# Sixty-eight columns transposed instead of 128, sixteen low halves made by DMA, and a re-costed planner in a fused attention + two-MLP kernel

## The chip, the cores and the metric

The kernel runs on one core of a Trainium2 chip. The metric is the device time of one execution in microseconds (us). Three runs of the kernel before gave 583.89, 578.93 and 583.06 us, median 583.06. A profile is one more execution, recorded instruction by instruction; its own time was 584.52 us, of which 582.6 us is the span from its first to its last instruction.

## The reference

Inputs are q, k, v of shape (2, 8, 768, 64) and four weight matrices. In short:

```
scores = q @ k^T / 8            # 2 batches, 8 heads, 768 x 768
keep   = (key < 4) | (0 <= query - key < 128)        # 4 sinks, a window of 128
x = softmax(where(keep, scores, -1e9)) @ v           # -> 1536 tokens x 512
h = x @ w_in1 ; x = (h * clip(h + 3, 0, 6) / 6) @ w_out1     # 512 -> 2048 -> 512
h = x @ w_in2 ; y = (h * sigmoid(1.702 h)) @ w_out2          # 512 -> 2048 -> 512
```

All inputs and outputs are float32. The weights are converted on the chip and every product of the MLPs is made of three products of rounded parts (high x high, high x low, low x high).

## The kernel before, in words

**Attention.** 1536 tokens are 12 tiles of 128 queries. A tile has two "duos" of four heads each (`duo`). Of one head a tile looks at 196 keys: 128 in the middle and a second part of 68 (64 of the window's ends plus 4 sinks). For a duo PE makes the scores (L1152), DVE adds the mask and takes the row's minimum of the negated scores (L1167, with a short read of the accumulator), ACT takes the exponential in place in a tile `pexp` (L1175, likewise two records), DVE makes the inverse sums (L1183, L1184), and DVE or ACT scales `pexp` (L1194, L1192). Then PE transposes: one "turn" (`turn`, L1203) turns two heads with four 128x128 transposes into one PSUM bank, and one copy of 128x512 (L442 on ACT, L444 on DVE) brings it to `pts` in SBUF. There are 48 turns. The tile `pexp` has 256 columns before; its last 60 are zeroed once at the start (L1100). `tile_values` multiplies by v (L1226 the 128 keys, L1234 the 68) and writes the result as a high part (ACT) and a low part (DVE, L1253) into `xy`.

**MLPs.** The work is a list of items; an item is one block of 512 tokens and one slice f of 128 hidden columns. Item i has an "up" (12 matmuls of 512 columns, L932) and a "down" (12 more, L980). The first layer's items come in the order of `BLOCKS`: tokens 0 to 511 with f 0 to 7 (items 0 to 7), tokens 512 to 1023 with f 0 to 7 (items 8 to 15), then f 8 to 15 of the same two blocks (items 16 to 31), then the last block. The second layer follows (items as before, then a part in a form with fewer products, L616 and L732). An item's activation is L944 on ACT and L949 on DVE, its split into high and low L442 or L444 and L565.

**Weights.** A slice f of both matrices arrives by a 1 MB DMA into one of two `stage` buffers and is converted by ACT (L472) and four DVE steps (L477, L485, L493, L500). The load of slice f+2 can start only when L500 of slice f has released the buffer. For each item W_in and W_out are then split: the high part is a cast (L442 on ACT or L444 on DVE), the low part is weight minus high part, a subtraction on DVE (L550): tile `w0l` for W_in, tile `wg` for W_out. The rings of W_out's high and low parts (`w1h`, `w1l`) have two buffers each, so the parts for item i can be made only when the down of item i-2 has finished.

**What sets the order.** A planner (`Plan.issue`) goes through all operations with an assumed cost for each on each engine that may do it, and writes every engine's instructions out in the order that it finds. On the chip an engine works strictly in that order. DMAs with accumulation are issued by POOL; before the change they are used only in the last part (L680, L824), with an assumed latency ADD_DMA of 4500 ns.

Of the kernel before, what the change touches and what calls it, by code (L numbers as in the profile page):

```python
# [9 lines left out]
F32 = mybir.dt.float32  # L10
# [4 lines left out]
ALU = mybir.AluOpType  # L15
PSUM = bass.MemoryType.PSUM

P = 128
SINKS = 4
HALF = 64  # L20
# [15 lines left out]
SLACK = 50  # L36
ISSUE = 1300
ADD_DMA = 4500
PACT = 0.15
PDVE = 0.5  # L40
STRETCH = 1.0
# [12 lines left out]
PX = 8  # L54
# [13 lines left out]
def tile_sink_window_attention_moe_moe2(  # L68
# [10 lines left out]
    nc = tc.nc  # L79
    B, S, H, D = 2, 768, 8, 64  # L80
    NTOK, DM = out.shape
    NF = w1.shape[0]
# [7 lines left out]
    TAIL = HALF + SINKS  # L90

    W = P + TAIL
# [81 lines left out]
    ident = const.tile([P, P], F32, name="ident")  # L174
# [58 lines left out]
    with tc.tile_pool(name="msk", bufs=1) as mp:  # L233
# [18 lines left out]
            out=out, in0=grid, scalar1=x, scalar2=LOW, op0=op, op1=ALU.mult  # L252
# [187 lines left out]
    def copy(eng, out, in_):  # L440
        if eng is nc.scalar:
            eng.copy(out, in_)  # L442
        else:
            eng.tensor_copy(out, in_)  # L444
# [20 lines left out]
    def plan_convert(plan, f, due):  # L465

        st, w = plan.stage[f % len(stage)], plan.wf[f]
        wd = st.tile.rearrange("p (n t) -> p n t", t=2)
        low, top = wd[:, :, 0], wd[:, :, 1]
        plan.op(  # L470
            [("ACT", 1036)],
            lambda e: e.activation(w.tile.bitcast(F32), top.bitcast(F32), AF.Abs),  # L472
            due, reads=[st], writes=[w], chain="abs",
        )
        plan.op(
            [("DVE", 602)],
            lambda e: e.tensor_scalar(  # L477
                out=w.tile.bitcast(F32), in0=w.tile.bitcast(F32), scalar1=TOP_LO, scalar2=TOP_HI,
                op0=ALU.max, op1=ALU.min,
            ),  # L480
            due, writes=[w],
        )
        plan.op(
            [("DVE", 602)],
            lambda e: e.tensor_scalar(  # L485
                out=w.tile, in0=w.tile, scalar1=3, scalar2=0x3FFFFFF8,
                op0=ALU.logical_shift_left, op1=ALU.bitwise_and,
            ),
            due, writes=[w],
        )  # L490
        plan.op(
            [("DVE", 1135)],
            lambda e: e.scalar_tensor_tensor(  # L493
                out=w.tile, in0=top, scalar=-0x40000000, in1=w.tile, op0=ALU.bitwise_and, op1=ALU.bitwise_or
            ),
            due, reads=[st], writes=[w],
        )
        plan.op(
            [("DVE", 1135)],
            lambda e: e.scalar_tensor_tensor(  # L500
                out=w.tile, in0=low, scalar=29, in1=w.tile, op0=ALU.logical_shift_right, op1=ALU.bitwise_or
            ),
            due, reads=[st], writes=[w],
        )


    def plan_mlps(plan, blocks, item_due, late=None):
# [13 lines left out]
        second = len(items) - NF  # L521
# [7 lines left out]

        def split(i, part):  # L530
            f = items[i][3]
            return split_of(plan.wf[f], slice(512 * part, 512 * (part + 1)), f"w{part}", part, i >= second - NF + 4)

        def split_of(src, cols, cls, part=0, act=True):
            hi, lo = Buf(cls=cls + "h"), Buf(cls=cls + "l")
            n = cols.stop - cols.start
            at = (slice(None), slice(None)) if part else (slice(None), slice(0, n))

            def of():
                x = src.tile if src.tile.dtype == F32 else src.tile.bitcast(F32)  # L540
                return parted(x[:, cols]) if part else x[:, cols]

            full = n == 512
            opts = [("ACT", 520 if full else 300)] + ([] if act else [("DVE", 335)])
            plan.op(
                opts, lambda e: copy(e, hi.tile[at], of()), None, reads=[src], writes=[hi], chain=f"split{part}",
            )
            plan.op(
                [("DVE", 602 if full else 335)],
                lambda e: e.tensor_tensor(  # L550
                    out=lo.tile[at], in0=of(), in1=hi.tile[at].bitcast(F32), op=ALU.subtract
                ),
                None, reads=[src, hi], writes=[lo],
            )
            return hi, lo
# [485 lines left out]
        for i in range(len(items)):  # L1041
            f = items[i][3]
# [9 lines left out]
            if second <= i < second + NF:  # L1052
                f = i - second
# [36 lines left out]
    def plan_attention(plan, pool, due):  # L1090
# [4 lines left out]
        kept = [pool.tile([P, KQ], F32, name="kept", tag=f"kept{j}") for j in range(KEPT)]  # L1095
        for T in range(EARLY, NTILE):
            kqt[T] = kept[T % KEPT]
        pexps = [pool.tile([P, 2 * P], F32, name="pexp", tag=f"pexp{k}") for k in range(PX)]
        for t in pexps:
            nc.scalar.mul(t[:, W:], ident[:, W - P :], 0.0)  # L1100
        plan.ring("pexp", PX, lambda k: pexps[k])
        top, low = slice(0, HALF), slice(HALF, P)
        both = slice(0, P)
# [1 line left out]
        kq_b = [Buf(kqt[T], at=landed.get(("kq", T))) for T in range(EARLY + KEPT)]  # L1105
# [16 lines left out]
        def duo(d, pts):  # L1122

            T, half = divmod(d, 2)
            i = tok[T][1]
            kind = min(i, 2)
            front = T - 1 if i else T
            when = None
            sc = [Buf(cls="bank", kind="s") for j in range(2)]
            nbs, z = [Buf(cls="nb") for _ in range(4)], Buf(cls="z")  # L1130
            pes = [Buf(cls="pexp") for _ in range(4)]

            def scores(e):
# [22 lines left out]
                                )  # L1156

            plan.op(
                [("PE", 1050)], scores, when, reads=[kq_b[t] for t in sorted({front, T})], writes=sc, chain="scores",
            )  # L1160
            heads = [(a, j) for a in range(2) for j in range(2)]
            for a, j in heads:
                n = 2 * a + j
                cols = slice(a * W, (a + 1) * W)
                plan.op(
                    [("DVE", 283)],
                    lambda e, j=j, n=n, cols=cols: e.tensor_tensor_reduce(  # L1167
                        out=pes[n].tile[:, :W], in0=sc[j].tile[:, cols], in1=masks[kind],
                        scale=-SCALE, scalar=LOWEST, op0=ALU.add, op1=ALU.min, accum_out=nbs[n].tile,
                    ),  # L1170
                    when, reads=[sc[j], mask_b[kind]], writes=[pes[n], nbs[n]],
                )
                plan.op(
                    [("ACT", 410)],
                    lambda e, n=n: e.activation(  # L1175
                        pes[n].tile[:, :W], pes[n].tile[:, :W], AF.Exp,
                        bias=nbs[n].tile, scale=-1.0, accum_out=z.tile[:, n : n + 1],
                    ),
                    when, reads=[nbs[n]], writes=[pes[n]], adds=[z], chain="exp",
                )  # L1180
# [16 lines left out]
            for a in range(2):  # L1197
                pt, pb = Buf(cls="bank", kind="t"), Buf(cls="pts")

                def turn(e, a=a, pt=pt):  # L1200
                    for n in range(4):
                        j, x = divmod(n, 2)
                        e.transpose(  # L1203
                            pt.tile[:, n * P : (n + 1) * P], pes[2 * a + j].tile[:, x * P : (x + 1) * P], ident
                        )

                plan.op([("PE", 440)], turn, when, reads=pes[2 * a : 2 * a + 2], writes=[pt], chain="turn")
                plan.op(
                    [("ACT", 478), ("DVE", 602)],
                    lambda e, pt=pt, pb=pb: copy(e, pb.tile, pt.tile.rearrange("p (n t) -> p n t", t=P)),  # L1210
                    when, reads=[pt], writes=[pb],
                )
                pts.append(pb)

        def tile_values(T, pts):
# [6 lines left out]
            def values(e):  # L1222
                for hp in range(NPAIR):
                    p = pts[hp].tile
                    for j in range(2):
                        e.matmul(  # L1226
                            av.tile[j * D : (j + 1) * D, hp * P : (hp + 1) * P],
                            rows.tile[:, 2 * hp + j, :], p[:, 2 * j, :],
                            start=(hp == 0), stop=False, skip_group_check=True,
                        )  # L1230
                    for c in range(2):
                        for j in range(2):
                            o = hp * P + c * HALF
                            e.matmul(  # L1234
                                av.tile[j * D : (j + 1) * D, o : o + HALF],
                                halves_of[c].tile[:TAIL, c, 2 * hp + j, :],
                                p[:TAIL, 2 * j + 1, c * HALF : (c + 1) * HALF],
                                start=False, stop=True, skip_group_check=True,
                            )

            plan.op(
                [("PE", 2000)], values, when, reads=list(dict.fromkeys([rows] + halves_of)) + pts, writes=[av],
            )
            blk, off = divmod(T, 4)
            dst = (slice(None), off // 2, slice(None), slice(off % 2 * P, (off % 2 + 1) * P))
# [15 lines left out]
        for T in range(NTILE):  # L1261
            pts = []
# [7 lines left out]
    def fast_path():  # L1270
        with tc.manual_schedule(), tc.tile_pool(name="mlp", bufs=1) as pool, tc.tile_pool(
# [23 lines left out]
            def limit(b, slots, o):  # L1295
# [15 lines left out]
                    return free > (1 - mine if v or t else 2 - mine)  # L1311
                if b.kind == "v":
                    return v == 0 or free > 2
                if b.kind == "t":

                    return t + sum(1 for x in plan.slots["pts"] if x is not None and x.left) < NPT
# [186 lines left out]
```

## Time and profile before

| | before |
|---|---|
| runs | 583.89, 578.93, 583.06 us; median 583.06 |
| profiled execution | 584.52 us; span 582.6 us |
| PE busy | 563.2 us (97%) |
| DVE busy | 456.8 us (78%) |
| ACT busy | 389.4 us (67%) |
| POOL busy | 54.2 us (9%) |
| first matmul of an up | 42.6 us |
| up of item 8 begins | 114.9 us |
| up of item 16 begins | 165.2 us |
| last turn and values of the attention end | about 213 us |

PE is a pipeline: the busy time of one matmul contains its passage through the array, so neighbours overlap, and a busy share of 97% does not say that nothing waits. The share is an average over a span in which the work changes: attention alone at first, then attention together with the first MLP's items, then MLP alone. What a saving on another engine is worth depends on the stage in which it falls.

### The profile page before, as it was taken

The numbers are of one execution on the slowest core, as the hardware profiler recorded it, in microseconds if no ns is written. First come the engines' busy times: TensorE is split into PE (matmuls) and PEld (weight loads), VectorE is DVE, ScalarE is ACT, GpSimd is POOL, SyncE is SP. The second block draws the span as 40 slices with busy tenths as digits, with TensorE's granted clock in tenths as the row PEclk, the third lists the DMA queues.
The fourth block names the chain that finished last, engine by engine and source line by source line (L and its number), as shares of the span: only waits on it lengthen the run. The fifth ranks groups of instructions, "written<-read, shape, count | busy, mean of one in ns | idle before, by whom it ended". The sixth has DMA issues, their size and how long they took to land.

```text
span 582.6 us, 11436 instructions
## 1 busy us (share of the span) xinstructions
PE 563.2 (97%) x4482; PEld 496.6 (85%) x4482; DVE 456.8 (78%) x951; ACT 389.4 (67%) x803; POOL 54.2 (9%) x62
## 2 busy tenths in 40 slices
PE   6989989999999999999999999999999999999996
PEld 6868867788788888888888888888888888999995
DVE  6799979998996556559999999993456665667784
ACT  5898756984746665457655678454478788768762
POOL 0000000000000000000000000000002344765000
PEclk9799999999999999999999999999999999999998
DMA  8984464145342000000445440420024567999512
GB/s 256 364 249 161 124 201 164 44 145 186 111 168 74 1 2 1 1 0 1 151 168 186 147 145 1 144 74 1 0 78 77 82 95 145 168 184 198 99 38 77
DMA packets 23468, 65.65 MB, mean 113 GB/s; under 512 B 2480, under 2 KB 10672, under 8 KB 19312
## 3 DMA queue, kind: packets, MB, share of 16 engines
q1 hardware_dynamic: 13360, 51.22, 26.7%
q0 software_dynamic: 10048, 13.63, 14.8%
q8 instruction: 37, 0.61, 0.4%
q14 instruction: 23, 0.19, 0.1%
HBM read 47.02 MB, written 3.15 MB: 86 GB/s over the span
## 4 chain that ended last, share of the span: by engine, by line
PE 80%; DVE 9%; ACT 4%; DMA 3%; issue 1%; DVEq 0%; SPq 0%
PE bank L980 24%; PE bank L932 24%; PE bank L732 13%; PE bank L616 13%; DMA stage<-in_w_dram 3%; PE bank L1203 2%; ACT pexp L1175 2%; PE bank L1152 2%; PE bank L1226 2%; DVE wf L500 1%; DVE wf L493 1%; PE bank L1234 1%; DVE pexp L1167 1%; DVE wg L550 1%; DVE wf L485 1%
## 5 line engine op out<-in xcount | busy, mean ns | idle before, releaser
L980 PE MATMUL bank<-wg 128*128 128x512 f32 x768 | 190.0, 382 | 2.7 <-ACT wg L442 2.5
L980 PEld LDWEIGHTS bank<-wg 128*128 128x128 f32 x768 | 143.3, 189 | 24.7 <-ACT wg L442 3.2
L932 PE MATMUL bank<-xy,w0h 128*128 128x512 f32 x512 | 154.1, 382 | 1.5 <-DVE xy L1253 1.0
L932 PEld LDWEIGHTS bank<-xy,w0h 128*128 128x128 f32 x512 | 95.5, 189 | 15.3 <-DVE xy L1253 1.3
L932 PE MATMUL bank<-xy,w0l 128*128 128x512 f32 x256 | 97.0, 379 | 0.0
L680 POOL DMA_DIRECT2D wf<-wf x24 | 29.0, 1287 | 469.2 <-ACT wf L661 433.9
L442 ACT CAST wg<-wf 128x512 fp32r<-128x512 f32 x78 | 48.2, 618 | 31.9 <-PE bank L980 24.4
L944 ACT ACTIVATE u<-bank,three 128x512 f32<-128x512 f32 x48 | 32.8, 684 | 39.4 <-PE bank L932 39.3
L550 DVE TENSOR_TENSOR w0l<-wf,w0h 128x512 fp32r<-128x512 f32 x72 | 49.2, 684 | 11.6 <-ACT w0h L442 11.4
L550 DVE TENSOR_TENSOR wg<-wf,wg 128x512 fp32r<-128x512 f32 x64 | 43.9, 685 | 15.3 <-ACT wg L442 15.3
L932 PEld LDWEIGHTS bank<-xy,w0l 128*128 128x128 f32 x256 | 48.4, 189 | 6.8
L949 DVE SCALAR_TENSOR_TENSOR u<-u,bank 128x512 f32<-128x512 f32 x48 | 32.7, 681 | 24.3 <-ACT u L944 24.1
L1175 ACT ACTIVATE pexp<-pexp,nb 128x196 f32<-128x196 f32 x96 | 42.9, 450 | 9.2 <-DVE nb L1167 8.9
L472 ACT ACTIVATE wf<-stage 128x1024 f32<-128x1024 f32 x32 | 37.8, 1182 | 16.2 <-DMA stage<-in_w_dram 12.9
L442 ACT CAST wg<-u 128x512 fp32r<-128x512 f32 x59 | 36.6, 620 | 14.3 <-DVE u L949 14.3
L565 DVE TENSOR_TENSOR wg<-u,wg 128x512 fp32r<-128x512 f32 x64 | 43.9, 685 | 0.9
L493 DVE SCALAR_TENSOR_TENSOR wf<-stage,wf 128x1024 int32<-128x1024 int32 x32 | 39.1, 1221 | 0.4
L500 DVE SCALAR_TENSOR_TENSOR wf<-stage,wf 128x1024 int32<-128x1024 int32 x32 | 39.0, 1219 | 0.2
L576 ACT ACTIVATE u<-bank 128x512 f32<-128x512 f32 x32 | 19.1, 596 | 30.1 <-PE bank L932 22.9
L616 PE MATMUL bank<-xy,w0h 128*128 128x512 f32 x128 | 38.1, 379 | 0.0
L442 ACT CAST w0h<-wf 128x512 fp32r<-128x512 f32 x60 | 36.7, 611 | 1.1 <-DVE wf L500 0.5
L1203 PE MATMUL bank<-ident,pexp 128*128 128x128 f32 x192 | 28.7, 289 | 5.6 <-DVE pexp L1194 2.8
(189 smaller groups left out, 996.0 us busy)
## 6 DMA issues: line engine op xcount, KB each, us to landing
stage<-in_w_dram SPq DMA_DIRECT2D x32, 1024.0 KB, 4.9
wf<-wf POOLq DMA_DIRECT2D x24, 256.0 KB, 3.9
wf<-in_kq_dram SPq DMA_DIRECT2D x8, 520.0 KB, 11.8
vc<-in_vc_dram SPq DMA_DIRECT2D x12, 320.0 KB, 6.1
vb<-in_v_dram SPq DMA_DIRECT2D x10, 256.0 KB, 6.5
kept<-in_kq_dram SPq DMA_DIRECT2D x4, 520.0 KB, 10.9
aside<-wf SPq DMA_DIRECT2D x4, 256.0 KB, 3.1
aside<-wf POOLq DMA_DIRECT2D x4, 256.0 KB, 5.1
```

Source lines behind the costliest of these rows:

```text
L442: eng.copy(out, in_)
L472: lambda e: e.activation(w.tile.bitcast(F32), top.bitcast(F32), AF.Abs),
L493: lambda e: e.scalar_tensor_tensor(out=w.tile, in0=top, scalar=-0x40000000, in1=w.tile, op0=ALU.bitwise_and, op1=ALU.bitwise_or),
L500: lambda e: e.scalar_tensor_tensor(out=w.tile, in0=low, scalar=29, in1=w.tile, op0=ALU.logical_shift_right, op1=ALU.bitwise_or),
L550: lambda e: e.tensor_tensor(out=lo.tile[at], in0=of(), in1=hi.tile[at].bitcast(F32), op=ALU.subtract),
L565: lambda e: e.tensor_tensor(out=gl.tile, in0=parted(u.tile), in1=gh.tile.bitcast(F32), op=ALU.subtract),
L616: e.matmul(bank.tile, l, woven(r), start=(begin and j == 0 and k == 0), stop=(j == 1 and k == 2), skip_group_check=True,)
L732: e.matmul(to, l, woven(t), start=(begin and n == 0 and m == 0 and e4 % share == 0), stop=(n == pairs - 1 and m == 2), skip_group_check=True,)
L932: e.matmul(h.tile[:, :n], w, woven(x), start=(c == 0 and k == 0), stop=(c == NC - 1 and k == 2))
L980: e.matmul(yb.tile, l, woven(r), start=(begin and k == 0), stop=(end is not None and k == 2))
L1175: lambda e, n=n: e.activation(pes[n].tile[:, :W], pes[n].tile[:, :W], AF.Exp, bias=nbs[n].tile, scale=-1.0, accum_out=z.tile[:, n : n + 1],),
L1203: e.transpose(pt.tile[:, n * P : (n + 1) * P], pes[2 * a + j].tile[:, x * P : (x + 1) * P], ident)
```

## The change

Three edits. First, of a head's second part of 68 keys only the 68 columns that hold anything are transposed: the input of two of a turn's four transposes is 128x68, the output 68x128; the zeroing of `pexp` goes, the bank is laid out with the two 128-key parts first, and the copy to `pts` becomes two copies of 256 columns each (128 and 68 partitions), each of which may go to ACT or DVE. Second, for items 0 to 15 the low part of W_out is made without DVE: ACT writes minus the high part (one operation of 128x512, L552 after) and a DMA issued by POOL (L555 after) adds the weight to it. Third, the planner's assumed costs change (conversion 1036 to 1062, scores 1050 to 900, exponential 410 to 443, turn 440 to 360, values 2000 to 1830) and a bank for an MLP result is not given out while four score banks are in use. The planner then finds another order.

```diff
+BY_DMA = 16
...
-            [("ACT", 1036)],
+            [("ACT", 1062)],
...
+            cols, by_dma = slice(512 * part, 512 * (part + 1)), bool(late and part and i < BY_DMA)
+            return split_of(plan.wf[f], cols, f"w{part}", part, i >= second - NF + 4, by_dma)
...
+            if by_dma:
+                plan.op(
+                    [("ACT", 520)], lambda e: e.mul(lo.tile, hi.tile.bitcast(F32), -1.0), None, reads=[hi], writes=[lo],
+                )
+                plan.op(
+                    [("POOL", ADD_DMA)], lambda e: e.dma_start(out=lo.tile, in_=of(), accum_op=ALU.add), None,
+                    reads=[src], writes=[lo],
+                )
+                return hi, lo
...
-        pexps = [pool.tile([P, 2 * P], F32, name="pexp", tag=f"pexp{k}") for k in range(PX)]
-        for t in pexps:
-            nc.scalar.mul(t[:, W:], ident[:, W - P :], 0.0)
+        pexps = [pool.tile([P, W], F32, name="pexp", tag=f"pexp{k}") for k in range(PX)]
...
                     for n in range(4):
-                        j, x = divmod(n, 2)
+                        x, j = divmod(n, 2)
+                        src = pes[2 * a + j].tile
                         e.transpose(
-                            pt.tile[:, n * P : (n + 1) * P], pes[2 * a + j].tile[:, x * P : (x + 1) * P], ident
+                            pt.tile[: TAIL if x else P, n * P : (n + 1) * P], src[:, P:W] if x else src[:, :P], ident
                         )
-                plan.op([("PE", 440)], turn, when, reads=pes[2 * a : 2 * a + 2], writes=[pt], chain="turn")
-                plan.op(
-                    [("ACT", 478), ("DVE", 602)],
-                    lambda e, pt=pt, pb=pb: copy(e, pb.tile, pt.tile.rearrange("p (n t) -> p n t", t=P)),
+                plan.op([("PE", 360)], turn, when, reads=pes[2 * a : 2 * a + 2], writes=[pt], chain="turn")
+                for x, rows in enumerate((P, TAIL)):
+                    def take(e, pt=pt, pb=pb, x=x, rows=rows):
+                        src = pt.tile[:rows, x * 2 * P : (x + 1) * 2 * P].rearrange("p (n t) -> p n t", t=P)
+                        copy(e, pb.tile[:rows, 2 * x : 2 * x + 2, :], src)
+                    plan.op(
+                        [("ACT", 300), ("DVE", 335)], take, when, reads=[pt],
+                        **(dict(adds=[pb]) if x else dict(writes=[pb])),
+                    )
...
+                if b.kind == "y":
+                    return used.count("s") < 4
```

The order on PE hardly changes: ups, downs, turns and values follow each other as before but for a few exchanges of neighbours. Two places on the engines that feed PE show what moved.

DVE, between the activation of item 3 and that of item 4 (the conversion of the next weight slice with its splits; `wg<-wf` is the low part of W_out, `w0l<-wf` that of W_in). Before:

```order
L477 TENSOR_SCALAR wf<-wf 128x1024
L444 CAST wg<-wf 128x2x256
L550 TENSOR_TENSOR w0l<-wf,w0h 128x512
L485 TENSOR_SCALAR wf<-wf 128x1024
L1167 ISA pexp,nb<-bank,mask_122 128x196
L1167 ISA nb 128x1
L1253 TENSOR_TENSOR xy<-bank,xy 128x4x128
L493 SCALAR_TENSOR_TENSOR wf<-stage_61,wf 128x1024
L550 TENSOR_TENSOR wg<-wf,wg 128x2x256
L500 SCALAR_TENSOR_TENSOR wf<-stage_61,wf 128x1024
```

After (all line numbers behind the added code are higher by 9 to 15):

```order
L445 CAST wg<-u 128x2x256
L445 COPY pts<-bank 68x256
L576 TENSOR_TENSOR wg<-u,wg 128x2x256
L445 CAST wg<-wf 128x2x256
L561 TENSOR_TENSOR w0l<-wf,w0h 128x512
L478 TENSOR_SCALAR wf<-wf 128x1024
L1176 ISA pexp,nb<-bank,mask_122 128x196
L1176 ISA nb 128x1
L486 TENSOR_SCALAR wf<-wf 128x1024
```

The subtraction `wg<-wf,wg` is gone from DVE; a copy of half a turn and a cast of an activation have come from ACT.

ACT, behind the sixth activation (L944), where the turns of one tile are copied out (`pts<-bank`). Before:

```order
L944 ACTIVATE u<-bank,three 128x512
L472 ACTIVATE wf<-stage_61 128x1024
L1192 ACTIVATE pexp<-pexp,z 128x196 x3
L442 CAST wg<-u 128x2x256
L442 COPY pts<-bank 128x512 x4
L442 CAST w0h<-wf 128x512
L442 CAST xy<-bank 128x4x128
```

After:

```order
L955 ACTIVATE u<-bank,three 128x512
L443 COPY pts<-bank 128x256
L1201 ACTIVATE pexp<-pexp,z 128x196 x2
L443 COPY pts<-bank 128x256
L443 COPY pts<-bank 68x256 x2
L443 CAST wg<-wf 128x2x256
L443 COPY pts<-bank 128x256
L552 ACTIVATE wg<-wg 128x2x256
L443 COPY pts<-bank 68x256 x2
```

Four copies of 512 columns have become seven of 256 here (the eighth is on DVE); the cast of the high part of W_out (`wg<-wf`) and the operation that writes minus that part (L552) stand among them. On POOL sixteen DMAs `wg<-wf` (L555) now stand ahead of everything that it issued before.

## Rows read from the trace of the kernel before

**Rows 1.** Busy by stretch: PE, PEld, DVE, ACT, POOL; clock, DMA share, GB/s.

```profile
0.00:42.60 42.60, 34.74 (x802) 30.73 (x802) 33.30 (x155) 33.01 (x107) 1.42 (x10) 0.88 0.89 291
42.60:114.90 72.30, 67.13 (x785) 55.72 (x785) 68.25 (x186) 54.15 (x135) 0.00 (x0) 1.00 0.45 141
114.90:165.20 50.30, 49.64 (x407) 42.46 (x405) 48.23 (x99) 32.33 (x69) 0.00 (x0) 1.00 0.46 155
165.20:213.60 48.40, 48.40 (x490) 41.45 (x489) 33.90 (x89) 31.41 (x77) 0.00 (x0) 1.00 0.15 49
213.60:582.60 369.00, 363.33 (x2005) 326.27 (x2003) 273.12 (x426) 238.47 (x416) 52.75 (x52) 1.00 0.39 89
```

**Rows 2.** Chain of waits, 70 to 82 us: start, length, what.

```profile
70.54 1.15 DVE wf L500
71.74 8.88 DMA stage<-in_w_dram
80.64 1.17 ACT wf L472
```

**Rows 3.** DVE timeline: start, length, instruction, idle before it and its releaser.

```profile
59.97 0.68 DVE L550 TENSOR_TENSOR wg<-wf,wg 128x512 fp32r<-128x512 f32 x1
60.58 0.41 DVE L444 CAST w0h<-wf 128x512 fp32r<-128x512 f32 x1
60.91 0.35 DVE L1167 CUSTOM_DVE_ANT_0 pexp<-bank,mask 128x196 f32<-128x196 f32 x1
...
81.84 0.69 DVE L477 TENSOR_SCALAR wf<-wf 128x1024 f32<-128x1024 f32 x1 [2.49 <-ACT wf L472]
```

**Rows 4.** DVE by line, 42.6 to 165.2 us: count | busy, mean ns | idle before.

```profile
L550 DVE TENSOR_TENSOR wg<-wf,wg 128x512 fp32r<-128x512 f32 x16 | 10.9, 682 | 1.3 <-ACT wg L442 1.3
L477 DVE TENSOR_SCALAR wf<-wf 128x1024 f32<-128x1024 f32 x13 | 8.8, 687 | 2.6 <-ACT wf L472 2.5
L1194 DVE TENSOR_SCALAR pexp<-pexp,z 128x196 f32<-128x196 f32 x28 | 7.6, 316 | 0.0
```

**Rows 5.** ACT by line, whole span: the rows nearest to the added operations.

```profile
L442 ACT COPY pts<-bank 128x512 f32<-128x512 f32 x45 | 24.4, 588 | 3.6 <-PE bank L1203 3.5
L661 ACT ACTIVATE wf<-wf 128x512 f32<-128x512 f32 x16 | 9.6, 625 | 0.0
L442 ACT CAST sh<-wf 128x256 fp32r<-128x256 f32 x8 | 3.3, 408 | 0.0
```

**Rows 6.** ACT timeline at the start: zeroing of pexp, the first exponential.

```profile
4.98 1.25 ACT L1100 ACTIVATE pexp<-ident 128x60 f32<-128x60 f32 x8 [2.75 <-DVE snk L251]
8.11 0.46 ACT L1175 ACTIVATE pexp<-pexp,nb 128x196 f32<-128x196 f32 x1 [1.87 <-DVE nb L1167]
```

**Rows 7.** DMA: issues with KB and us to landing; POOL's queue; L680's landing.

```profile
wf<-wf POOLq DMA_DIRECT2D x24, 256.0 KB, 3.9
q0 software_dynamic: 10048, 13.63, 14.8%
DMA to landing us min/median/max: 3.3/5.5/12.8
```

**Rows 8.** PE timeline: the down of item 8, and the start of item 10's.

```profile
122.08 2.75 PE L980 MATMUL bank<-wg 128*128 128x512 f32 x12
130.95 0.81 PE L980 MATMUL bank<-wg 128*128 128x512 f32 x3
```

**Rows 9.** Chain of waits: two turns, and the values of one group.

```profile
204.62 0.87 PE bank L1203 x8
...
25.82 0.22 PE bank L1226 x4
```

**Rows 10.** PE's weight loads by line: count | busy, mean ns | idle before.

```profile
L1203 PEld LDWEIGHTS bank<-ident,pexp 128*128 128x128 f32 x192 | 23.0, 147 | 10.4 <-issue 2.7 <-ACT pexp L1192 2.4 <-ACT pts L442 1.2
L1226 PEld LDWEIGHTS bank<-pts,vb 128*64 128x64 f32 x192 | 10.3, 144 | 4.2 <-issue 2.8 <-ACT pexp L1175 0.3 <-ACT wg L442 0.3
```

**Rows 11.** POOL timeline: its first DMA.

```profile
434.62 1.34 POOL L680 DMA_DIRECT2D wf<-wf  x1 [432.63 <-ACT wf L661]
```

More of the change, by code (lines that the diff above doesn't have):

```diff
@@ L531, in split, with split_of @@
             f = items[i][3]
-            return split_of(plan.wf[f], slice(512 * part, 512 * (part + 1)), f"w{part}", part, i >= second - NF + 4)
-        def split_of(src, cols, cls, part=0, act=True):
+            cols, by_dma = slice(512 * part, 512 * (part + 1)), bool(late and part and i < BY_DMA)
+            return split_of(plan.wf[f], cols, f"w{part}", part, i >= second - NF + 4, by_dma)
+        def split_of(src, cols, cls, part=0, act=True, by_dma=False):
             hi, lo = Buf(cls=cls + "h"), Buf(cls=cls + "l")
@@ L1158, in duo @@
             plan.op(
-                [("PE", 1050)], scores, when, reads=[kq_b[t] for t in sorted({front, T})], writes=sc, chain="scores",
+                [("PE", 900)], scores, when, reads=[kq_b[t] for t in sorted({front, T})], writes=sc, chain="scores",
             )
@@ L1173, in duo @@
                 plan.op(
-                    [("ACT", 410)],
+                    [("ACT", 443)],
                     lambda e, n=n: e.activation(
@@ L1201, in turn @@
                     for n in range(4):
-                        j, x = divmod(n, 2)
+                        x, j = divmod(n, 2)
+                        src = pes[2 * a + j].tile
                         e.transpose(
-                            pt.tile[:, n * P : (n + 1) * P], pes[2 * a + j].tile[:, x * P : (x + 1) * P], ident
+                            pt.tile[: TAIL if x else P, n * P : (n + 1) * P], src[:, P:W] if x else src[:, :P], ident
                         )
-                plan.op([("PE", 440)], turn, when, reads=pes[2 * a : 2 * a + 2], writes=[pt], chain="turn")
-                plan.op(
-                    [("ACT", 478), ("DVE", 602)],
-                    lambda e, pt=pt, pb=pb: copy(e, pb.tile, pt.tile.rearrange("p (n t) -> p n t", t=P)),
-                    when, reads=[pt], writes=[pb],
-                )
+                plan.op([("PE", 360)], turn, when, reads=pes[2 * a : 2 * a + 2], writes=[pt], chain="turn")
[7 more added lines that the diff above has]
+                    )
                 pts.append(pb)
@@ L1227, in values @@
                             av.tile[j * D : (j + 1) * D, hp * P : (hp + 1) * P],
-                            rows.tile[:, 2 * hp + j, :], p[:, 2 * j, :],
+                            rows.tile[:, 2 * hp + j, :], p[:, j, :],
                             start=(hp == 0), stop=False, skip_group_check=True,
@@ L1236, in values @@
                                 halves_of[c].tile[:TAIL, c, 2 * hp + j, :],
-                                p[:TAIL, 2 * j + 1, c * HALF : (c + 1) * HALF],
+                                p[:TAIL, 2 + j, c * HALF : (c + 1) * HALF],
                                 start=False, stop=True, skip_group_check=True,
@@ L1241, in tile_values @@
             plan.op(
-                [("PE", 2000)], values, when, reads=list(dict.fromkeys([rows] + halves_of)) + pts, writes=[av],
+                [("PE", 1830)], values, when, reads=list(dict.fromkeys([rows] + halves_of)) + pts, writes=[av],
             )
```

## The prediction, as it was put on record

> **What bounds the kernel now.** I read the busy time by stretch first, cut where the program's stages change [rows 1]. PE is busy 34.74 of the first 42.6 us, 67.13 of the next 72.3 (items 0 to 7), 49.64 of 50.3 (items 8 to 15), 48.40 of 48.40 until the last values, and nearly back to back in the remaining 369 us. So the change, which touches the attention and items 0 to 15, can earn something only before 165.2 us, and of PE's idle time there is 5.17 + 0.66 = 5.83 us behind 42.6 us, plus what the start holds. In 42.6 to 114.9 DVE is busy 68.25 of 72.3 us, ACT 54.15: PE waits for a DVE that has next to no slack. From 114.9 on PE is the bound, with DVE at 48.23 of 50.3 a close second; in 165.2 to 213.6 DVE works 33.90 of 48.40 and has room.
>
> Next the chain of waits around DVE's longest idle time [rows 2]: L500 of one weight slice ends, its stage buffer is free, a load of 8.88 us follows, then L472 on ACT, and only then can DVE go on: 2.49 us idle before L477 [rows 3]. DVE's saving is worth something only outside such a stall.
>
> **Prices.** A busy time of DVE holds the passage through the engine, which the next instruction overlaps; what counts is start to start. A two-input operation of 128x512 takes 60.58 - 59.97 = 0.61 us against 0.68 shown, a cast 60.91 - 60.58 = 0.33 against 0.41 [rows 3]; both lose 0.07 to 0.08. So I take L1194 as 0.316 - 0.08 = 0.23 us [rows 4], and a slice's two-input step of 1024 columns as 1.14, since L500 shows 1.15 [rows 2]. The copy of half a turn (256 columns out of PSUM) is not in the trace: at least half of 0.61, that is 0.30, if a copy of a whole turn costs what the widest class of 512 columns costs, at most 0.61 if halving saves nothing. I take 0.33, the cast's price. On ACT a whole copy shows 0.59 busy, and an SBUF cast of 256 columns 0.41 [rows 5]; half a turn lies between 0.29 and 0.59, and I take the nearest row's 0.41 less an overlap like DVE's, 0.33. The operation that writes minus the high part is one of 0.62 as L661 [rows 5].
>
> **The sum for DVE**, from the order of its instructions, activation of item 0 to that of item 8:
>
> - 9 low parts of W_out go: -9 x 0.605 = -5.45.
> - L1194 falls from 18 to 8 (ACT scales those): -2.3.
> - one `w0l` falls behind the cut: -0.6.
> - 4 casts of an activation and one of a weight come over from ACT: +5 x 0.335 = +1.68.
> - 4 half copies: +1.34 (2.4 at the upper price).
> - the last two steps of a later weight slice come before the cut instead of behind it: +2.28.
>
> Together -3.05 us (-2.0 with dear half copies). From item 8 to 16: six low parts less, -3.63; four more row minima with their mask, +1.12; two casts of `w0h`, three half copies, a `w0l`, two L1194 and small ones, less two casts of an activation, +2.4: together -0.1. Between items 16 and 17 DVE has 3.3 less, where PE is the bound. Before item 0 DVE gets 0.55 more (eight half copies for two whole ones, less three L1194 and a subtraction).
>
> **What of it arrives.** Items 0 to 7: DVE is the bound, so -3.05 arrives, less what the stall takes. Between L500 of the slice that frees the buffer and L477 of the slice that waits [rows 2, 3] DVE had 7.66 us of other work and now has 7.4: the load does not care, so the stall grows by 0.25. Items 8 to 15: nothing. The start: eight zeroing operations leave ACT (1.25 us), but they lie ahead of an exponential that waits 1.87 us for DVE's row minimum [rows 6], so they are hidden; if that cover were gone they would cost 1.25. DVE's +0.55 there stands in a stretch in which it is busy 33.30 of 42.6 us and the DMA engines 0.89 [rows 1]; I give it half, +0.3. After 165.2 nothing. Sum: +0.3 - 3.05 + 0.25 - 0.1 = about **-2.7 us**.
>
> **ACT** gets 5.2 us more in items 0 to 7 (nine operations of minus the high part, eleven scalings that were L1194's and 28 half copies for 16 whole ones, less the casts given to DVE) and 3.6 in items 8 to 15. 54.15 of 72.3 and 32.33 of 50.3 [rows 1] leave 18 us of cover each; if that were gone, the 5.2 would be paid in full. I cost it at nothing in the middle, and it is part of the range's upper end.
>
> **The DMA's own path.** Cast of the high part 0.62, minus the high part 0.62, then issue to landing. Transfers of the same size and kind land in 3.9 us at the median, those of L680 in 3.3 to 12.8 with a median of 5.5 [rows 7]: 5.1 us in all, up to 14.0. The parts for item 10 can be begun when the down of item 8 leaves the buffer (122.08 + 2.75 = 124.83) and are wanted at 130.95 [rows 8]: 6.1 us, the shortest I found. It just fits. The 16 transfers are hidden work for the 16 DMA engines: POOL's queue took 14.8% of 582.6 us for its 52 [rows 7], 1.66 us each, 26.5 us in all over 122.6 us, which lifts the DMA share from 0.45 to about 0.67. Sixteen issues on POOL cost nothing: it is idle until 434.62 [rows 11].
>
> **The shorter turns on PE.** Two turns take 0.87 us for eight transposes, 109 ns each [rows 9]; the identity, 128 columns, streams through an array loaded with `pexp`. That stream keeps its 128 columns. A product of the values with a loaded block half as wide, 64 columns, streams 128 as well and takes 0.22 for four, two at a time [rows 9]: 110 ns per pass. The weight loads themselves show 147 ns for 128 columns and 144 for 64 [rows 10]. So a block of 68 instead of 128 should save nothing. Bounds: nothing, or at most the share of the columns, 96 transposes x 109 x 60/128 = 4.9 us, of which only the 32 behind 114.9 us (1.6 us) fall where PE is the bound. I take nothing.
>
> The Trainium skill, page "TensorE: Matmul & The Clock Gate", section "LDWEIGHTS (loading the stationary operand)", says that a load takes about its column count over 1.2 ns: by that an estimate of 57 against 107 ns, which would make a transpose shorter if loads set the pace, and the sum that of the third rival below. The weight loads here, 147 and 144 ns [rows 10], do not show that halving.
>
> **Time.** The profiled execution took 584.52 us (span 582.6, 1.9 around it), 1.46 above the median of the runs, 583.06. 584.52 - 2.7 = 581.8 for such an execution; on the median **580.4**.
>
> **The rivals.**
>
> - *DMA contention lengthens the stage loads* (0.17). A load that takes 8.88 us beside a DMA share of 0.45 shares the engines with 26.5 us more. For it: 2.49 us of stall hang on one such load already [rows 2, 3]. Against it: only about one accumulating DMA falls into each load. One more of 1.66 us in the way makes the stall that much longer, at one place or two: 582 to 583.7, say 582.5.
> - *All of PE's idle time behind 42.6 us goes* (0.12): if shorter DVE work unties every wait, 5.83 us [rows 1]: 577.2. Against it is the stage load, which no DVE saving shortens.
> - *The turns do get shorter on PE* (0.06): the 1.6 us above on top of the forecast, 578.8.
> - *Slower: POOL's issues and DVE's one-input operations get into each other's way* (0.12). If a DMA's issue on POOL and L477, its neighbour of the same shape and L1194 can't go on at once, an issue of 1.2 to 1.34 us [rows 11] meets them for the share of time that they hold, (8.8 + 8.8 + 7.6)/122.6 = 0.21 [rows 4], or makes DVE wait its whole length where it meets one: up to 16 x 1.3 x 0.21 = 4.4 us of DVE, and as much again of POOL and its landings. It decides once more than 2.7 us of that falls on DVE: 580.4 + 4.4 = 584.8 or so. The trace of before can't tell: POOL issues nothing before 434.62 [rows 11].
> - *Slower: the accumulating DMA lands late* (0.08). With two buffers an item's pair repeats every 12.6 us on average in items 8 to 15 (50.3/4), less a down of 2.75 [rows 8]: 9.8 us for a path of 1.24 plus landing. It decides above 8.6 us of landing on average (4.9 at item 10 alone). At the slowest landing shown, 12.8 [rows 7], each of four pairs is 4.2 us late: about 597.
>
> The Trainium skill, page "SBUF — State Buffer", section "Who interferes with whom", says that GpSimd and VectorE share a port and hold each other off in VectorE's faster modes, which would be a ground for the fourth rival. No run here shows it yet.
>
> The forecast itself gets 0.45. The range holds forecast, contention, PE's whole idle time, the turns and most of the port case, 576.0 to 586.0; dearer half copies (+1.0) and ACT's 5.2 in part lie inside, late landings and a full port loss outside.
>
> One per cent, 5.8 us, is about what a measurement of this kernel can tell from no change. Faster than 577.2 needs all idle time and something at the start or in the turns: 0.16, half of the third case and the upper tail of the others. Slower than 588.9: late landings, 0.08, and a little for ports: 0.09. The rest, 0.75, is within 1%.
>
> **What would show it.** Busy by stretch: items 0 to 7 should last about 69.5 us instead of 72.3, with DVE still above 90%, and items 8 to 15 about 50.3. The stage load behind L500 should still take 8 to 9 us; 10.5 or more there means contention. PE waiting for `wg` with a DMA as releaser means late landings. L477 and L1194 longer than 687 and 316 ns on the mean, beside POOL's issues, mean ports. Two turns below 0.87 us mean that the 68 columns count on PE. The forecast is wrong if the stretch of items 0 to 7 does not shrink, or if the stretch before 42.6 us moves by more than 1 us.

## The result, and the profile after

| | before | after |
|---|---|---|
| median of 6 runs each | 584.12 us (578.93 to 584.65) | 589.44 us (587.72 to 593.12) |
| ratio | | 1.0119, 95% interval 1.0088 to 1.0150 |
| span of the profiled run | 582.6 us | 588.2 us |

The change is slower by 1.2%: 5.3 us by the medians, 6.9 us by the ratio. The forecast of 580.4 us was wrong, and the time lies above its range.

The first view is again busy time by stretch, cut at the same events as [rows 1]: first matmul of an up, up of item 8, of item 16, of item 23, end. Before, these events stand at 42.64, 114.85, 165.21 and 213.55 us when read to the hundredth. Columns: stretch and its length, busy us (instructions) of PE, PE's weight loads, DVE, ACT and POOL, the granted clock, the DMA share, GB/s.

```profile
0.00:43.72 43.72, 35.94 (x802) 30.61 (x803) 33.85 (x161) 31.98 (x112) 2.54 (x11) 0.88 0.86 281
43.72:114.71 70.99, 66.28 (x785) 55.53 (x785) 66.11 (x177) 58.96 (x160) 10.35 (x9) 1.00 0.68 181
114.71:171.87 57.16, 51.63 (x458) 43.98 (x453) 47.30 (x98) 37.11 (x82) 8.79 (x7) 0.97 0.63 173
171.87:219.25 47.38, 47.38 (x447) 40.85 (x442) 32.60 (x90) 29.52 (x78) 0.00 (x0) 1.00 0.12 40
219.25:588.20 368.95, 363.52 (x2005) 326.38 (x2003) 272.65 (x425) 238.90 (x417) 52.56 (x52) 1.00 0.39 89
```

The start is 1.1 us longer than before, items 0 to 7 are 1.2 us shorter (70.99 against 72.21), items 8 to 15 are 6.8 us longer (57.16 against 50.36), the stretch behind them 1.0 shorter (48.34 before), since one group of scores (0.86 us) now stands ahead of the cut. So the loss lies in items 8 to 15, where PE had idled 0.66 us and now idles 5.53. The chain of waits there says where (start, length, what):

```profile
143.26 2.59 PE bank L943 x12
145.85 0.41 PE bank L991 x2
146.25 10.32 DMA wg<-wf
156.57 0.04 issue
156.62 1.22 PE bank L991 x2
157.84 1.28 PE bank L943 x3
159.12 0.92 PE bank L991 x3
```

One accumulating DMA, that of item 13, took 10.32 us from issue to landing (the arrival of its data), and item 13's down waited for it: PE has run one matmul of it, waits 5.53 us and goes on at 156.62. The next rows of the chain are long, too: three matmuls of L943 take 1.28 us, which take 0.65 elsewhere. The stretches around them (columns as above) show why:

```profile
150.00:156.60 6.60, 1.09 (x6) 0.60 (x4) 4.63 (x16) 3.00 (x9) 1.20 (x1) 0.96 1.11 309
156.60:160.20 3.60, 3.58 (x10) 2.96 (x11) 0.00 (x0) 0.00 (x0) 0.00 (x0) 0.59 0.53 218
```

Behind its idle time PE got a clock of 0.59 for 3.6 us, near the lower of its two levels: another 3.6 x 0.41 = 1.5 us. (By the chain it is 1.7: eight matmuls take 1.22 + 1.28 + 0.92 us, and at 0.65 for three they take 1.73 elsewhere.) Together the one landing costs 7.0 us by this estimate. Without it this execution would have been 1.4 us shorter than the profiled one of before.

What was in flight: POOL's own timeline and then the DMA queue's (SPq, the loads) around it.

```profile
139.13 1.38 POOL L555 DMA_DIRECT2D wg<-wf  x1 [6.79 <-PE bank L943]
146.25 1.37 POOL L555 DMA_DIRECT2D wg<-wf  x1 [5.74 <-ACT pexp L1201]
150.35 1.20 POOL L555 DMA_DIRECT2D wg<-wf  x1 [2.73 <-ACT wg L552]
```

```profile
147.24 0.33 SPq L120 DMA_DIRECT2D stage<-in_w_dram  x1
149.41 0.33 SPq L126 DMA_DIRECT2D kept<-in_kq_dram  x1
153.38 0.33 SPq L120 DMA_DIRECT2D stage<-in_w_dram  x1
```

While POOL still issues the DMA (146.25 to 147.62), a weight slice of 1 MB starts (147.24), then keys and queries of 520 KB, the next accumulating DMA, and another slice. The DMA share of 150.00 to 156.60 us is 1.11 (a mean of summed packet times, so it can pass 1), where it was 0.46 on the mean of items 8 to 15 before [rows 1]. The landing of all 16:

```profile
DMA to landing us min/median/max: 3.8/4.6/10.3
```

### The profile page after: what moved, and what is told of

Its sections match the earlier page's. It is cut to its first block, busy times and chain, and to the rows that moved or that the text cites. A ratio compares the mean times of both kernels' runs of the same rounds, so it can differ in the third digit from the quotient of the medians.

```text
span 588.2 us, 11535 instructions
## 1 busy us (share of the span) xinstructions
PE 564.7 (96%) x4482; PEld 497.4 (85%) x4482; DVE 452.5 (77%) x947; ACT 396.5 (67%) x847; POOL 74.2 (13%) x78
## 4 chain that ended last, share of the span: by engine, by line
PE 86%; DVE 6%; DMA 4%; issue 1%; ACT 1%; DVEq 0%; SPq 0%
PE bank L991 26%; PE bank L943 26%; PE bank L743 13%; PE bank L627 12%; PE bank L1213 3%; DMA stage<-in_w_dram 3%; PE bank L1161 2%; PE bank L1241 2%; DMA wg<-wf 2%; PE bank L1249 2%; DVE wf L501 1%; DVE pexp L1176 1%; DVE wf L494 1%; DVE u L960 1%; DVE wf L478 0%
## 5 line engine op out<-in xcount | busy, mean ns | idle before, releaser
L943 PE MATMUL bank<-xy,w0h 128*128 128x512 f32 x512 | 154.9, 384 | 1.1 <-DVE xy L1268 1.0
L943 PEld LDWEIGHTS bank<-xy,w0h 128*128 128x128 f32 x512 | 95.6, 190 | 15.2 <-DVE xy L1268 1.3
L943 PE MATMUL bank<-xy,w0l 128*128 128x512 f32 x256 | 97.3, 380 | 0.0
L943 PEld LDWEIGHTS bank<-xy,w0l 128*128 128x128 f32 x256 | 48.5, 190 | 6.9
L473 ACT ACTIVATE wf<-stage 128x1024 f32<-128x1024 f32 x32 | 37.9, 1185 | 14.8 <-DMA stage<-in_w_dram 13.9
L561 DVE TENSOR_TENSOR wg<-wf,wg 128x512 fp32r<-128x512 f32 x48 | 32.9, 686 | 14.3 <-ACT wg L443 14.2
L555 POOL DMA_DIRECT2D wg<-wf x16 | 20.3, 1267 | 144.9 <-ACT wg L552 77.7
L443 ACT CAST w0h<-wf 128x512 fp32r<-128x512 f32 x57 | 34.9, 613 | 2.3 <-DVE wf L501 1.8
## 6 DMA issues: line engine op xcount, KB each, us to landing
wf<-in_kq_dram SPq DMA_DIRECT2D x8, 520.0 KB, 11.5
kept<-in_kq_dram SPq DMA_DIRECT2D x4, 520.0 KB, 11.2
```

Of the source, the lines that this page charges most:

```text
L561: lambda e: e.tensor_tensor(out=lo.tile[at], in0=of(), in1=hi.tile[at].bitcast(F32), op=ALU.subtract),
L943: e.matmul(h.tile[:, :n], w, woven(x), start=(c == 0 and k == 0), stop=(c == NC - 1 and k == 2))
```

## The experiments

Theory L says that one DMA landed late beside weight loads and cost the time. Rivals: O, the new order itself costs the time; B, POOL and DVE hold each other off. Each ratio is to runs of the kernel before on the same chip (582.2 to 583.0 us at the median), in 5 rounds, eighth14 and the two slow kernels with fewer runs.

| kernel | us | ratio (95%) |
|---|---|---|
| pool_add13 | 582.43 | 0.9998 (0.9973 to 1.0024) |
| pool_add | 588.51 | 1.0098 (1.0059 to 1.0137) |
| by13 | 581.02 | 0.9971 (0.9947 to 0.9995) |
| by0 | 582.04 | 0.9993 (0.9972 to 1.0015) |
| by8 | 582.06 | 1.0006 (0.9985 to 1.0027) |
| eighth14 | 581.99 | 0.9977 (0.9953 to 1.0001) |
| lat9 | 590.27 | 1.0117 (1.0084 to 1.0150) |
| dma_only | 583.25 | 1.0003 (0.9981 to 1.0024) |
| turn_only | 585.02 | 1.0032 (1.0013 to 1.0051) |
| costs_only | 580.28 | 0.9959 (0.9944 to 0.9974) |
| costs_dma8 | 580.49 | 0.9970 (0.9954 to 0.9986) |
| costs_dma13 | 581.67 | 0.9987 (0.9967 to 1.0007) |
| low8 | 580.70 | 0.9972 (0.9954 to 0.9990) |
| costs_low8 | 579.82 | 0.9961 (0.9943 to 0.9978) |

**pool_add13: item 13's addition without a DMA.** Every engine's order is as in the changed kernel.

```diff
-lambda e: e.dma_start(out=lo.tile, in_=of(), accum_op=ALU.add)
+lambda e: e.tensor_tensor(out=lo.tile, in0=of(), in1=lo.tile.bitcast(F32), op=ALU.add)   # item 13 only
```

> The changed kernel, with every engine's order as it is, but for item 13 alone the accumulating DMA is one POOL instruction that adds the weight to minus the high part (128x512). Theory L (late landing: the one DMA issued at 146.25 us that landed 10.3 us later stopped PE for 5.53 us and the clock fell for some us behind it, together about 7.2 us by the trace): the wait at item 13's down goes; item 14's DMA, which landed 10.0 us after its issue, may then be late by up to 2.5 us. 582 to 585 us. Rival O (the new order of the instructions costs the time, the landing only marks where): 588 to 590 us, PE waits for something else at that place. Rival B (POOL's compute instruction and DVE hold each other off): above 590 us.

582.43 us, ratio 0.9998: 1.2% or 7 us off the changed kernel's 1.0119, and no PE wait for a DMA is left. L holds; O falls, since no engine's order changed.

**pool_add: the same for all 16 items.**

> The same for all 16 items: no accumulating DMA before the last part, order unchanged, POOL adds. Theory L: no PE wait on a DMA at any down of items 0 to 15, 581 to 583 us. Rival O: 588 to 590 us. Rival B: DVE's two-input or one-input operations beside POOL's get longer than 0.69 us, and the time stays above 585 us.

588.51 us: no wait for a DMA, and yet nothing won. DVE by line, 40 to 180 us, of this kernel (count, busy, mean ns, idle before):

```profile
L486 DVE TENSOR_SCALAR wf<-wf 128x1024 int32<-128x1024 int32 x15 | 12.1, 808 | 0.1
L1192 DVE TENSOR_SCALAR z<-z 128x4 f32<-128x4 f32 x13 | 5.4, 415 | 0.0
L445 DVE CAST wg<-u 128x512 fp32r<-128x512 f32 x6 | 3.2, 541 | 0.0
```

and of the changed kernel:

```profile
L486 DVE TENSOR_SCALAR wf<-wf 128x1024 int32<-128x1024 int32 x15 | 10.5, 700 | 0.1
L1192 DVE TENSOR_SCALAR z<-z 128x4 f32<-128x4 f32 x13 | 2.1, 162 | 2.2 <-ACT pexp L1184 2.2
L445 DVE CAST wg<-u 128x512 fp32r<-128x512 f32 x6 | 2.5, 421 | 0.0
```

Three of the 13 tiny operations of L1192 met a POOL instruction and took 1.24 to 1.26 us instead of 0.16. Summed over all DVE instructions that meet one of POOL's sixteen, the excess over the same instruction alone is about 11.7 us. This is rival B, true for POOL's arithmetic and not for its DMAs: beside the 16 DMA issues the same sum is about 0.3 us. In items 0 to 7 DVE is busy 73.51 us here, 66.11 in the changed kernel, and the stretch takes 76.02 us instead of 70.99. So as a test of L over all items this kernel failed: it took one cost away and put another in. The Trainium skill, page "SBUF — State Buffer", section "Who interferes with whom", calls the shared port pair an exclusive lock between VectorE and GpSimd that blocks fully; the 0.16 us operation at 1.26 us beside POOL's addition agrees. The prediction's use of it for DMA issues is not borne out by the 0.3 us.

**by13, by8, by0: DMAs for the first 13, 8 or no items.**

```diff
-BY_DMA = 16
+BY_DMA = 13        # by8: 8, by0: 0
```

> The changed kernel with the accumulating DMA for items 0 to 12 only; items 13 to 15 make the low part on DVE as before (the planner's order changes a little from there on). Theory L: no wait of 5 us at item 13's down, 581 to 584 us. Rival O: 587 us or more.

> The changed kernel with accumulating DMAs for items 0 to 7 alone, the stretch in which DVE is the bound. If those behind item 8 only bring the risk of a late landing: 579 to 582 us, no PE wait for a DMA. If DMAs for items 8 to 12 earn something too: about 1 us above the 581.0 us of items 0 to 12.

> The changed kernel without any accumulating DMA for these items: the 68-column turn, the split copies and the new planner costs alone. Theory L: no stall of 5 us, but DVE keeps 16 subtractions of 0.605 us, of which 9 in the stretch where it is the bound: 583 to 588 us. Rival O: as slow as the changed kernel, 588 to 590 us, since the order is what costs.

581.02, 582.06 and 582.04 us. Without the DMAs of items 13 to 15 the changed kernel is 0.3% faster than before, by an interval that ends just below 1; L holds. by0 lies below the 583 to 588 us that L gave it. by8 and by0 differ by nothing, so eight DMAs where DVE was thought the bound earn nothing on top of the new order. by13 stands 1.0 us below both, as by8's second branch had it, but the intervals overlap. The planner finds another order for each of the three, so these are comparisons of orders, too; only pool_add13 and eighth14 keep the order of the changed kernel.

**eighth14: the neighbour in flight made small.** Slice 14's load, 1 MB, becomes 128 KB.

```diff
-dma_start(out=stage[f % len(stage)], in_=w[f])
+dma_start(out=stage[f % 2][:, :256], in_=w[f][:, :256])   # for slice 14 of the first layer
```

This kernel leaves out the other seven eighths of the slice. The code is shortened.

> The changed kernel, order unchanged, but the weight slice whose load was issued at 147.24 us (slice 14 of the first layer), 1.0 us behind item 13's accumulating DMA, is loaded to one eighth (the rest of the slice is left out, so its numbers are old ones). Theory C (the DMA landed late because that load and the 520 KB one behind it shared the 16 DMA engines with it): item 13's DMA lands in 4 to 7 us instead of 10.3, PE's wait there falls from 5.5 to under 2.5 us, 582 to 585 us. Rival P (the landing is long on its own: POOL's issue, its descriptors, or accumulating itself): 10 us again, PE waits 5 us again, 588 to 590 us.

581.99 us. Landings of its 16 accumulating DMAs, and who waited for them:

```profile
  PEld bank L991: 0.3, 1
...
DMA to landing us min/median/max: 3.8/4.3/7.3
```

Item 13's landed 4.7 us after its issue (146.94 to 151.64), and PE's matmuls did not wait: the one wait listed, 0.3 us, is of PEld, PE's own load of its array. The load beside it made it late: theory C holds, rival P falls. It fits by little, since PE wants the data 4.8 us after the issue here, too. Over the nine profiled kernels with such DMAs there are 121 landings. Counting the weight loads in flight between the end of POOL's issue and the landing, they take 3.78 to 4.30 us for the 16 with none, 4.5 at the median with one (up to 7.7), 5.7 with two (up to 10.3); the shortest of each group is 3.78. The Trainium skill, page "DMA: Bandwidth & Descriptors", section "Queues, rings and completion order", has each DMA engine take turns between its queues, packet by packet; these landings fit, and nothing here shows the packets' order.

**lat9: a longer latency in the planner.**

```diff
-[("POOL", ADD_DMA)]
+[("POOL", 9000)]      # the 16 DMAs alone
```

> The changed kernel with an assumed latency of 9000 ns instead of 4500 for the 16 accumulating DMAs, so that the planner orders around it. If a late landing is what costs: no wait of more than 2 us for such a DMA at a down, 580 to 583 us. If the planner's order under contention can't be mended so: a wait of several us at another item, 585 us or more.

590.27 us. Half a miss: no wait for a DMA is left, as hoped, but the order that the planner then finds is as slow: items 0 to 7 take 74.4 us (two groups of scores more among them, some 1.8 us) and items 8 to 15 52.9, with PE waiting for copies of turns and activations instead. A planner that is told a long landing gives up as much for the sixteen as the one late one costs.

**dma_only, turn_only, costs_only: one edit each on the kernel before.**

> The kernel before with the 16 accumulating DMAs alone: old turns, old planner costs. Theory L: DVE's relief shows unless one of the 16 DMAs falls beside a 1 MB load with less than its landing to spare: 579 to 582 us if none does, 585 to 590 us with one such wait in the trace. Rival D (DVE's relief is worth nothing since ACT takes its place): 583 to 585 us without any wait for a DMA.

> The kernel before with the 68-column turn and the split copies alone, old planner costs. A transpose stays at 109 ns, so PE gains nothing; half copies cost DVE and ACT together some us more than whole ones: 583 to 586 us. If the shorter turn does help: under 581 us.

> The kernel before with the planner's new costs and the new rule for a result's bank alone; whole turns of 128 columns and whole copies, no accumulating DMA. The 68-column turn alone took 2 us more than the kernel before, the turn and the new costs together 0.9 us less. If the two add, the new costs alone give about -3 us: 579 to 581 us. If the costs only suit the split copies: 582 to 585 us.

583.25, 585.02 and 580.28 us. The DMAs alone give nothing. PE waits for none of them, and the time is rival D's; that ACT is the reason is not shown. The turn costs 2.0 us (0.32% by the ratio), the new costs give 2.0 (0.41%), and both together, by0, give 0.9993; costs_only is faster than both kernels. Where turn_only loses was not tried apart; the work that its edit adds is in the copies. From start to start a whole copy of a turn takes ACT 0.477 us and DVE 0.601, two halves 2 x 0.263 and 2 x 0.337.

**costs_dma8, costs_dma13: DMAs on top of the costs, whole turns.**

> The kernel before with the new planner costs and accumulating DMAs for items 0 to 7 alone (the stretch in which DVE is the bound), whole copies of the turns. If DVE's relief counts there and no DMA lands beside a stage load with too little to spare: 577 to 580 us. If the relief is worth nothing: as the new costs alone.

> The kernel before with the new planner costs and accumulating DMAs for items 0 to 12, whole copies of the turns. Two half copies take ACT 0.526 us from start to start and DVE 0.674, a whole one 0.477 and 0.601; with the same DMAs as the 581.0 us kernel this one has some 2 to 3 us less work on ACT and DVE in the attention: 578 to 581 us. If a DMA lands late in this order: 585 us or more, with PE waiting for it.

580.49 and 581.67 us. costs_dma8 came out as the new costs alone, its second branch: the DMAs earn nothing on top of them. costs_dma13 is a miss, and in it another wait appears. Its chain (start, length, what):

```profile
131.47 9.49 DMA stage<-in_w_dram
140.96 0.02 issue
140.99 1.15 ACT wf L473
142.14 0.58 ACT u L955
...
145.02 2.08 PE bank L991 x4
147.10 1.18 PE bank L943 x3
```

Here it is the weight load that is stretched, to 9.49 us (7.80 for the same slice before); two accumulating DMAs, another slice and two value loads are in flight with it. ACT stands 4.44 us at L473 for it, the activation of an item queues behind, PE idles 2.06 us and then runs at the lower clock. It is the forecast's first rival, with the price that the clock adds.

**low8, costs_low8: DVE's relief by itself.** The subtraction is made for 8 of 512 columns in items 2 to 15; nothing takes its place.

```diff
-out=lo.tile[at], in0=of(), in1=hi.tile[at]
+out=lo.tile[:, :, :4], in0=of()[:, :, :4], in1=hi.tile[:, :, :4]   # items 2 to 15
```

> The kernel before, its order unchanged, but for items 2 to 15 the low part of W_out is made for 8 of its 512 columns (the other 504 are left out): about 0.5 us of DVE less for each, 3.5 us in items 0 to 7, and neither a DMA nor an ACT operation instead. Theory B (DVE bounds items 0 to 7, as the forecast said): that stretch falls by about 3 us and the time to 579.5 to 580.5 us. Rival S (the stage loads or ACT bound it): under 1 us, 582 to 583 us.

> The same on the kernel with the new planner costs alone (580.3 us). PE's idle time in items 0 to 7 was 1.2 us there, against 5.1 in the kernel before. If relief and order draw on the same idle time: 579.3 to 580.3 us, a gain of no more than 1 us. If they add: 577 to 578 us.

580.70 and 579.82 us: 1.5 us for the relief on the old order (interval 0.6 to 2.7), between theory B's and rival S's figures; on the new one 0.5 by the medians of two sessions and nothing by the ratios (0.9961 against 0.9959). Items 0 to 7 by stretch, of low8 and of costs_low8 (columns as at the top):

```profile
42.60:113.05 70.45, 67.15 (x784) 56.77 (x784) 65.09 (x186) 54.13 (x135) 0.00 (x0) 0.98 0.44 144
```

```profile
44.71:112.12 67.41, 66.27 (x784) 56.99 (x784) 63.07 (x180) 52.95 (x134) 0.00 (x0) 0.97 0.45 148
```

and of costs_only and dma_only:

```profile
44.65:112.56 67.91, 66.72 (x785) 57.23 (x785) 66.12 (x180) 52.70 (x134) 0.00 (x0) 0.97 0.45 147
```

```profile
44.38:112.92 68.54, 66.73 (x737) 55.99 (x737) 64.75 (x172) 55.99 (x139) 9.99 (x8) 0.98 0.67 190
```

PE's idle time in items 0 to 7 was 5.1 us before; the relief alone leaves 3.3, the costs alone 1.2, both together 1.1, the DMAs alone 1.8. They draw on the same 5 us, and with the new costs hardly any is left. But in the three kernels with another order the first up begins 1.7 to 2.1 us later (44.38 to 44.71 us), and PE idles longer ahead of it. Counted from the start to the up of item 8 PE idles 13.0 us before, 12.3 in low8, 11.2 in costs_only, 11.5 in costs_low8 and 11.5 in dma_only: half or more of what these orders save in items 0 to 7 is lost ahead of them.

In low8 eight of the shortened subtractions fall into items 0 to 7. Each takes 0.08 us from start to start instead of 0.60, so DVE is relieved of 4.2 us there and of 7.3 in all. The stretch shrinks by 1.8, that of items 8 to 15 by 1.5 (50.36 to 48.90), where the forecast saw nothing to gain. The stall before L477, 2.49 us in [rows 3], is still 2.0, and PE's clock fell: behind a wait of 1.65 us a down of 12 matmuls took longer than the same one before. From PE's timelines of low8 and of before:

```profile
82.85 4.55 PE L980 MATMUL bank<-wg 128*128 128x512 f32 x12 [1.65 <-ACT wg L442]
```

```profile
84.77 3.21 PE L980 MATMUL bank<-wg 128*128 128x512 f32 x12 [2.51 <-ACT wg L442]
```

The granted clock over these 12 was 0.70 in low8 and 1.00 before, and they took 1.3 us longer. All four rows above show 0.97 or 0.98, the one of before 1.00 [rows 1], so the lengths of these stretches hold such losses, too, and the runs are the better measure.

## Why the prediction was wrong, point by point

- **The late landing, given 0.08, is what happened; the step that failed is the landing that it put into its margin.** The prediction took the landing at its median of [rows 7], 3.9 us, against 4.9 us of room at the narrowest place ("It just fits"), although its own upper figure did not fit, and let the rival decide "above 8.6 us of landing on average". It needs no average. In the order after, item 11's down ends at 143.26 and item 13's second matmul wants the data at 151.1: 7.8 us. ACT's two operations and its queue took 3.0 until the issue at 146.25, which leaves 4.8; the landing took 10.3. One of 16 landings was late by 5.5 us, and PE, back to back there, passed all of it on to the end. The room was sized about right. What failed is the landing put into it: the forecast asked what the DMAs do to the weight loads and not what the loads do to the DMAs. From issue to want the changed order has two narrow places, item 13 with 4.8 us and item 10 with 5.2. Item 10's DMA landed in 3.80; that the two loads met item 13 and not item 10 could be seen only in the changed order.
- **The clock** was in no term: 1.5 us behind the wait, by the estimate above.
- **DVE's relief** was priced at 3.05 us for items 0 to 7, and the stretch shrank by 1.2 in the profile. One profile can't settle it: by13, eighth14 and pool_add13 have the same order on PE, DVE and ACT up to item 8, and theirs lasted 67.49, 69.45 and 72.21 us, at a granted clock of 1.00, 0.98 and 0.95. The runs are clearer. With the late landing gone the whole change gives 0.9998 (pool_add13) or 0.9977 (eighth14), and the forecast's 2.7 us, 0.9954, is outside the first interval and at the edge of the second. The work did go (DVE is busy 2.05 us less there), but a stretch in which DVE is busy 94% is not bound by DVE at each moment: alone on the old order a relief of 7.3 us, 4.2 of it in items 0 to 7, gave 1.5 by the runs (low8). With the DMAs and ACT's operations it earns nothing (dma_only). That the new costs' order would use up the same idle time was not considered at all; the forecast took the planner's change to be movement without worth, and it is the one part of the three that gains.
- **The stall** was to grow by 0.25 us, with a stage load of 8 to 9 us behind L500. That slice's load took 4.81 us in the changed kernel, and the longest wait of L478 (L477 before) for a load is 0.45 us instead of 2.49. So neither the term nor the sign for contention, 10.5 us or more, came there; why the load took 8.88 before stays open.
- **The start**: +0.3 forecast, +1.1 seen. In the profiles of the new orders the first up begins at 42.8 to 45.6 us, before at 42.6; one profile each, while whole runs of the kernel before lie 5.7 us apart (578.93 to 584.65). In the changed kernel's own profile a slice loaded at 38.4 took 9.55 us, in that of by13 5.8 with the same order. How much of it is the order stays open.
- **Right**: turns stay at 109 ns, as the chain and the weight loads after show; the loads of 68 columns do get shorter, 118 ns against 146, and the turn does not. That the turn's edit earns PE nothing was right; that it costs 2 us by itself (turn_only) was not foreseen. The forecast costed ACT's half copies at nothing; whether they are what costs the 2 us is not shown.

```profile
210.32 0.87 PE bank L1213 x8
```

```profile
L1213 PEld LDWEIGHTS bank<-ident,pexp 128*128 128x128 f32 x96 | 12.8, 146 | 9.8 <-issue 3.4 <-ACT pexp L1201 2.8 <-PE bank L1213 1.0
L1213 PEld LDWEIGHTS bank<-ident,pexp 128*68 128x68 f32 x96 | 11.2, 118 | 0.5 <-issue 0.4
```

- **Right in size**: half a copy on DVE 0.337 us from start to start (0.33 taken), minus the high part 0.63 (0.62), DMA share 0.68 and 0.63 (0.67). Half a copy on ACT is 0.263 (0.33 taken). Not borne out: POOL's issues against DVE (4.4 us as the bound, about 0.3 measured). The forecast's own sum, +0.3 - 3.05 + 0.25 - 0.1, is -2.6 and not -2.7, which changes nothing.

## What to carry to other kernels

A DMA put into the chain that feeds a busy engine has to be costed by its landing beside the largest load that can be in flight with it, at the narrow places of the new order, not by a median; one late landing of sixteen cost 7 us here. Where several edits relieve the same stall, price the idle time once: what the first one takes, the second can't. A saving on an engine that is 94% busy is worth what runs with that saving alone show, here 1.5 of 7.3 us. And two profiles of the same order can differ in one stretch by more than the effect that is looked for, here 67.49 to 72.21 us.

## What the runs showed of the hardware

- A 256 KB accumulating DMA from SBUF to SBUF lands in 3.8 to 4.3 us with no weight load in flight and in up to 10.3 us beside two of 1 MB (and one of 520 KB). With one of the two made 128 KB it landed in 4.7 us.
- A POOL addition of 128x512 (1.53 us) made a DVE operation of 0.16 us last up to 1.26 us, and sixteen of them cost DVE about 11.7 us; sixteen DMA issues on POOL (1.27 us each) cost it about 0.3.
- After 5.5 us of idling, PE ran 3.6 us at a granted clock of 0.59; in low8 a wait of 1.65 us was followed by 12 matmuls at 0.70, while before a wait of 2.51 us at the same place was followed by 12 at 1.00.
- Splitting a PSUM copy of 512 columns in two costs 0.05 us on ACT and 0.07 on DVE each time.
